# Groups of 256 tokens from the fourth on, and seven products over all 24 inner blocks

## The chip, the cores and the metric

The kernel runs on one core of a Trainium2 chip. The time is the device time of one execution in microseconds, and the time given for a kernel is the median of its runs. One execution is also recorded by the hardware profiler; its span runs from the first to the last instruction.

The core has five engines that run in parallel, each through its own instructions in order. TensorE (PE in the profile; PEld is its weight load) multiplies matrices into PSUM. VectorE (DVE), ScalarE (ACT) and GpSimd (POOL) work elementwise. SyncE (SP) issues DMA transfers and transposes; some transfers are issued from POOL.

## The reference

```python
# attention: q, k, v are (8, 12, 448, 64)
attn = np.maximum(q @ k.T / 8, 0) ** 2 / 448
x    = (attn @ v), heads side by side              # (8, 448, 768)
# mixing and feed-forward
u    = x + real(fft(fft(x, axis=1), axis=2))
un   = (u - mean(u)) / sqrt(var(u) + 1e-6)         # over the last axis
out  = u + np.maximum(un @ w_ch1, 0) @ w_ch2       # w_ch1 (768, 3072), w_ch2 (3072, 768)
```

There are 8 x 448 = 3,584 tokens of 768 channels. The 3,072 inner columns of the feed-forward part are 24 blocks of 128. The inputs and the output are float32; the matmuls take bfloat16 and accumulate in float32.

## The kernel before

**A planner writes the order.** The kernel is a set of Python generators, called streams. Each yields, with `need`, an engine, an estimated duration, the events it depends on (a `Cell` each) and the buffers it takes. `Streams.run` picks the stream that can start first (ties by rank) and lets it emit its instructions. So the order of each engine's instructions is fixed when the program is built, from estimates, and the hardware then runs every engine's list in that order, waiting where a semaphore says so.

**Attention and mixing, batch by batch.** TensorE makes score blocks (L588) into the three double banks `psS`; ACT takes their relu (L612) and VectorE squares them in place (L618); TensorE multiplies four squared blocks with v (L573) into one of the two banks `psF`. VectorE scales the result out of the bank (L474, L478), folds it (L497 to L511), and TensorE applies the Fourier matrices (L1034, L865). q and k of batches 2 and up are copied by VectorE (L412, one buffer each) and transposed by a DMA on SP (L424). The mixed rows u go to memory, their normalised form un too (`n_store`), and a DMA transpose on SP (L971 in `turn_un`) brings un back with channels on partitions, as `unT`. How far attention may run ahead is tied to the progress of the feed-forward part (`lead`, `APART`), so that TensorE always has both kinds of work until the last batch is mixed.

**Feed-forward, group by group.** `GT` cuts the tokens into groups: 384, 512, 384, 512, 256, 512, 512, 512. For a group of N tokens, `ffn` first makes the 24 inner blocks: for each block six matmuls of N columns (L1225) into a `psF` bank, and a relu by ACT (L1203) into `hT`, which has room for 24 x 512 columns and exists once. A bank holds 512 columns, so at N = 256 two blocks share a bank and a relu. When half the blocks are done, the loads of u into the output tiles `o` may start (L1167 in `outputs`, six slots). The second layer multiplies `hT` with the second weights for each tile of 128 tokens and each half of the 768 channels; VectorE adds the result to `o` (L1212), and SP stores `o` (L1171).

**Seven products for eight.** In groups 0 to 2 (`PLAIN`) the second layer is a plain sum over 24 blocks (L1256). From group 3 on it takes two 128-token tiles L and R together, a `Pair`, and treats two tiles by two halves of the inner blocks by two channel halves as a 2 x 2 matrix product that needs seven products instead of eight. An even and an odd inner block form the inner halves, so `KP` = 8 means that 16 of the 24 blocks are handled so; the other 8 are added the plain way (`rest`). A pair thus takes 7 x 8 + 4 x 8 = 88 matmuls of 384 columns (L1312).

This needs sums of rows and sums of weights. `early` makes s1, s2 and a difference in place for each pair on VectorE (L1293, L1295, L1297), in the portions `CH`, as the blocks arrive; `late` (L1305) makes one more, after chain b's first product has read the old value. `weight_sums` makes T1 to T4 once on VectorE (L1115), at the lowest rank; T3 lies in `unT0`, T2 in the former homes of u, T4 in former homes of squares, q and k, and T1 replaces a part of the second weights, so it must wait until group 2 has used them (`w2_free`). s1 and s2 lie in former homes of un, their last portion in `warm`.

`chain_a` and `chain_b` are two streams that alternate on TensorE, one bank each. A product goes into the bank on top of the former ones, and between products VectorE adds the bank's content to one of the `o` tiles. A relu of the next group may write `hT` only after both chains are done.

**Homes of `unT`.** Group 2 is transposed into `unT0`; groups 1 and 3 to 7 use `unT1`, so the transposes for one group wait for the first layer of the group before it. `turn_un(b)` runs inside the stream `mixes`, after the mix of batch b.

Of the kernel before, what the change touches and what calls it, by code (L numbers as in the profile page):

```python
# [142 lines left out]
def kernel(  # L143
# [27 lines left out]
    GT = [0, 384, 896, 1280, 1792, 2048, 2560, 3072, B * S]  # L171
    NGR = len(GT) - 1
    KP = 8
# [791 lines left out]
    def turn_un(b):  # L965

        def turn(g, c0, src, r0, w, deps, bufs=()):
            e = yield need("SP", 1.5, deps, bufs)
            if g is None:
                g = work.tile([128, MC, 512], BF16, name="unT", tag=f"unT{int(len(groups) != 2)}", bufs=1)  # L970
            nc.sync.dma_start_transpose(out=g[:, :, c0:c0 + w], in_=src[r0:r0 + w, :])  # L971
            return g, sch.dma(e + 0.5, w * D * 2, 180e3)

        if b == 1:
            yield need("SP", 0.0, second_un)
            e = max(c.t for c in second_un)
            BUN[0].free.append(e)
            BUN[1].free.append(e)
            group_ready[1].t = e
            return  # L980

        for k in range(2, NGR):
            if (GT[k + 1] - 1) // S != b:
                continue
            t, g = GT[k], None
            while t < GT[k + 1]:
                bb, r = divmod(t, S)
                src, half, r0 = (ntop[bb], 0, r) if r < HS else (nbot[bb], 1, r - HS)
                w = min(HS - r0, GT[k + 1] - t)
                g, e = yield from turn(g, t - GT[k], src, r0, w, n_stored[bb][half::2], [BUNT] if g is None else [])  # L990
                t += w
            groups.append((GT[k], GT[k + 1] - GT[k], g))
            group_ready[k].t = e

# [23 lines left out]
    def mix(b):  # L1018
# [39 lines left out]
        for ch in range(2):  # L1058
            if b > 0:
                sch.add(mix_rows(b, ch, pcs), (1, 1))  # L1060
            else:
                if ch == 0:
                    sch.add(first_tail(pcs), (0, 0))
                sch.add(first_stores(ch), (1, 1))
        if b > 0:
            yield from turn_un(b)
            return
# [13 lines left out]
    CH = [(0, 6), (6, KP)]  # L1081
# [10 lines left out]
    def weight_sums():  # L1092
# [34 lines left out]
        t4 = []  # L1127
        for tag, dep in ((f"sq{NSQ - 2}", sq_left), (f"sq{NSQ - 1}", sq_left), ("qn0", qk_left), ("kn0", qk_left)):
            t4 += yield from home(tag, 2, [dep])
# [50 lines left out]
    def ffn(b):  # L1180
# [4 lines left out]
        h = hid[0]  # L1185
# [22 lines left out]
        def add(pc, e, c, hf, last=True, give=True):  # L1208

            e = yield need("DVE", dve(DH), [e + LATENCY["PE"], ot[b, c, hf]])  # L1210
            o = os[b, c, hf]
            nc.vector.tensor_tensor(o, pc[:, 0:DH], o, op=ALU.add)  # L1212
            if give:
                BF.give(pc, e)
            if last:
                added[b, c, hf].t = e + LATENCY["DVE"]
            return e + LATENCY["DVE"]
# [18 lines left out]
        if b == 2:  # L1236
            unt_left.t = e
        else:
            BUNT.free.append(e)

        if b not in PLAIN:
            for p in pairs:
                sch.add(p.chain_a(), (4, 0))
                sch.add(p.chain_b(), (4, 0))
# [20 lines left out]
    class Pair:  # L1265
# [4 lines left out]
        def __init__(self, b, c, h, ht, add, advance):  # L1270
            self.b, self.c, self.h, self.ht, self.add, self.advance = b, c, h, ht, add, advance
            self.L, self.R = slice(c * 128, c * 128 + 128), slice(c * 128 + 128, c * 128 + 256)
            self.ev = [slice(2 * i0, 2 * i1, 2) for i0, i1 in CH]
            self.od = [slice(2 * i0 + 1, 2 * i1, 2) for i0, i1 in CH]
            self.r12, self.r4 = ([Cell() for _ in CH] for _ in range(2))
            self.m2, self.done = Cell(), [Cell(), Cell()]
            self.reads = Cell(), Cell()
            self.waits, Pair.read = Pair.read, [self.reads[0], self.reads[1], *self.r4]

        def early(self):  # L1280

            h, L, R_ = self.h, self.L, self.R
            if not made:
# [3 lines left out]
                ab = work.tile([128, 2, 2, 128], BF16, name="s3", tag="warm", bufs=1)  # L1287
                made.extend([[a1, ab[:, 0]], [a2, ab[:, 1]]])
# [19 lines left out]
        def product(self, pc, lhs, rhs, start, n=DH):  # L1308

            k = len(lhs)  # L1310
            for i in range(k):
                nc.tensor.matmul(pc[:, 0:n], lhsT=lhs[i], rhs=rhs[i], start=(start and i == 0),  # L1312
                                 stop=(i == k - 1), skip_group_check=True)
            self.advance(k * mm(n))

        def rest(self, pc, cols, hf, start):

            js = range(2 * KP, JC)
            self.product(pc, [self.h[:, j, cols] for j in js], [w2(j, hf) for j in js], start)
# [13 lines left out]
        def chain_a(self):  # L1333

            c, d, dr = self.c, KP * mm(DH), (JC - 2 * KP) * mm(DH)
            s1_read, s2_read = self.reads
            e = yield need("PE", d, self.ht[:2 * KP], [BF])
            pc = BF.take()
            self.product(pc, self.block(0, self.L), self.weights(0, 0), True)
            t = yield from self.add(pc, e, c, 0, False, False)  # L1340
# [3 lines left out]
            t = yield from self.add(pc, e, c + 1, 0, False, False)  # L1344
# [3 lines left out]
            t = yield from self.add(pc, e, c + 1, 1, False, False)  # L1348
# [6 lines left out]
        def chain_b(self):  # L1355

            c, d, dr = self.c, KP * mm(DH), (JC - 2 * KP) * mm(DH)
            e = yield need("PE", d + dr, self.ht, [BF])
            pc = BF.take()
            self.product(pc, self.block(1, self.L), self.weights(1, 0), True)  # L1360
            self.rest(pc, self.L, 0, False)
# [5 lines left out]
            t = yield from self.add(pc, e, c + 1, 1, False, False)  # L1367
            e = yield need("PE", d + dr, [t, sums[4]])
            self.product(pc, self.block(1, self.R), T[4], False)
            self.rest(pc, self.R, 0, False)  # L1370
            yield from self.add(pc, e, c + 1, 0)
            e = yield need("PE", dr, [], [BF])
            pc = BF.take()
            self.rest(pc, self.R, 1, True)
            self.done[1].t = e
            yield from self.add(pc, e, c + 1, 1)
# [20 lines left out]
    with tc.manual_schedule():  # L1397
# [13 lines left out]
        sch.add(weight_sums(), (6, 6))  # L1411
        for slot in range(6):
# [33 lines left out]
```

## Time and profile before

| | before |
|---|---|
| median of 3 runs | 599.19 us (599.04 to 600.49) |
| the profiled execution | 599.02 us |
| its span | 597.2 us |
| granted clock of TensorE | 1.000 |
| busy: PE, DVE, ACT, POOL | 583.0, 390.7, 292.5, 156.4 us |

Group 3's first layer starts at 275.6 us of the span. The last attention work ends near 479 us; what follows is feed-forward alone. In the rows below, a line such as `L1225 PE MATMUL psF<-unT,w 128*128 128x512` is a group of instructions of one source line, engine and shape, with its count, its busy time and the mean duration of one, and after the second bar the idle time before them and what ended it. A row of the chain gives a start, a length and what ran, and the chain follows the work that ended last back in time. A row of waits names who waited for whom: us in total, times, longest. A row of the timeline starts with start and duration.

### The profile page before, as it was taken

Reading aid. Unit: us, or ns where it says so; the run is one execution under the profiler, and the core shown is the slowest. Engines: PE = TensorE matmul, PEld = TensorE weight load, DVE = VectorE, ACT = ScalarE, POOL = GpSimd, SP = SyncE. Lnnn points to the kernel's source line nnn. Section 1 sums busy time; section 2 is a strip of 40 time slices with the busy share of each in tenths; the row PEclk is TensorE's granted clock in tenths of the full one; section 3 lists DMA queues with packets and bytes.
Section 4 is the critical chain, followed back from the end, with each engine's and each line's share of the span. In section 5 each row is a group of like instructions: output and inputs, shape, how many; then the busy total and the mean of one; then the engine's idle time right before and its main releaser. Section 6 shows DMA issues by size and latency. Waiting matters only on the chain.

```text
span 597.2 us, 10407 instructions
## 1 busy us (share of the span) xinstructions
PE 583.0 (98%) x3962; PEld 321.8 (54%) x3982; DVE 390.7 (65%) x889; ACT 292.5 (49%) x433; POOL 156.4 (26%) x200
## 2 busy tenths in 40 slices
PE   8999999989999999999989999999999999999997
PEld 7566556534455565555435667554355544654464
DVE  6977775865587767968857779757967481431043
ACT  5967661568545557534764147546743144004400
POOL 8433112311154135213531145114500062000000
PEclk9999999999999999999999999999999999999999
DMA  9999999974939989996598828974542133422021
GB/s 128 207 209 228 213 218 139 196 106 69 178 109 212 177 108 256 162 159 130 132 169 133 150 108 187 162 141 134 136 92 83 49 125 106 126 69 64 1 70 63
DMA packets 133361, 82.23 MB, mean 138 GB/s; under 512 B 77376, under 2 KB 128480, under 8 KB 133312
## 3 DMA queue, kind: packets, MB, share of 16 engines
q0 software_dynamic: 40320, 34.07, 35.7%
q1 hardware_dynamic: 92992, 47.50, 34.8%
q8 instruction: 31, 0.51, 0.3%
q14 instruction: 18, 0.15, 0.1%
HBM read 62.91 MB, written 26.69 MB: 150 GB/s over the span
## 4 chain that ended last, share of the span: by engine, by line
PE 85%; DVE 6%; ACT 3%; SPq 2%; DMA 2%; issue 1%; POOL 0%; DVEq 0%; ACTq 0%; POOLq 0%
PE psF L1225 32%; PE psF L1312 22%; PE psF L1256 13%; PE psF L573 6%; PE psS L588 6%; PE psS L1034 2%; ACT sq L612 2%; DVE sq L618 2%; PE psS L865 1%; SPq L1167 1%; DMA qkT<-qkr 1%; PE psS L664 1%; DVE stats L900 1%; PE psS L1009 1%; DVE u L887 0%
## 5 line engine op out<-in xcount | busy, mean ns | idle before, releaser
L1225 PE MATMUL psF<-unT,w 128*128 128x512 bf16 (+2 forms) x1132 | 226.2, 352 | 5.4 <-DVE xT L478 2.0
L612 ACT ACTIVATE sq<-psS 112x896 bf16<-112x896 f32 x192 | 164.9, 916 | 84.9 <-PE psS L588 82.0
L1225 PEld LDWEIGHTS <-w 128*128 128x128 bf16 x1152 | 109.4, 98 | 114.0 <-issue 13.9
L1203 ACT ACTIVATE hT<-psF 128x512 bf16<-128x512 f32 (+1 forms) x168 | 96.7, 576 | 127.9 <-PE psF L1225 124.7
L618 DVE TENSOR_TENSOR sq<-sq 112x896 bf16<-112x896 bf16 x192 | 121.9, 651 | 37.5 <-ACT sq L612 36.8
L1212 DVE TENSOR_TENSOR o<-psF,o 128x384 f32<-128x384 f32 x92 | 50.9, 554 | 70.6 <-PE psF L1312 67.6
L1312 PEld LDWEIGHTS <-hT 128*128 128x128 bf16 x648 | 62.9, 98 | 43.6 <-issue 2.1
L1312 PE MATMUL psF<-w,hT 128*128 128x384 bf16 x504 | 85.7, 326 | 0.0
L1256 PE MATMUL psF<-w,hT 128*128 128x384 bf16 x480 | 82.1, 326 | 0.0
L1256 PEld LDWEIGHTS <-hT 128*128 128x128 bf16 x480 | 45.5, 98 | 34.0 <-issue 5.7
L588 PE MATMUL psS<-qkT 64*112 64x448 bf16 x384 | 52.4, 366 | 1.4 <-ACT qkT L452 0.4
L319 POOL DMA_DIRECT2D vn<-in_v_dram x24 | 17.3, 721 | 120.0 <-PE psF L573 108.9
L573 PE MATMUL psF<-sq,vn 112*64 112x448 bf16 x384 | 45.5, 358 | 0.5 <-ACT hT L1203 0.5
L885 POOL TENSOR_TENSOR u<-tp,xn 128x385 f32<-128x385 f32 (+1 forms) x14 | 13.2, 942 | 97.3 <-DVE tp L874 89.8
L474 DVE TENSOR_SCALAR xT<-psF 128x224 bf16<-128x224 f32 x48 | 18.4, 384 | 28.4 <-PE psF L573 28.4
L917 POOL TENSOR_SCALAR un<-u,rstd,nmr 128x768 bf16<-128x768 f32 (+1 forms) x24 | 28.7, 1199 | 28.9 <-DVE nmr L909 26.3
L588 PEld LDWEIGHTS <-qkT 64*112 64x112 bf16 x384 | 20.8, 125 | 26.9 <-issue 21.0
L573 PEld LDWEIGHTS <-vn 112*64 112x64 bf16 x384 | 17.8, 109 | 22.7 <-issue 14.1
L319 POOL DMA_DIRECT2D qn<-in_q_dram x21 | 15.2, 721 | 50.3 <-DVE qkr L412 41.8
L900 DVE BATCH_NORM_STATS2 stats<-u 128x6 f32<-128x384 f32 (+1 forms) x56 | 28.2, 539 | 0.0
L1312 PE MATMUL psF<-wsum,hT 128*128 128x384 bf16 x144 | 26.4, 326 | 0.0
L942 POOL DMA_INDIRECT ubot<-u,back x16 | 16.9, 1056 | 23.9 <-ACT hT L1203 19.7
(137 smaller groups left out, 496.9 us busy)
## 6 DMA issues: line engine op xcount, KB each, us to landing
out_dram<-o SPq DMA_DIRECT2D x56, 192.0 KB
vn<-in_v_dram POOLq DMA_DIRECT2D x24, 224.0 KB, 5.0
qn<-in_q_dram POOLq DMA_DIRECT2D x21, 224.0 KB, 5.0
kn<-in_k_dram POOLq DMA_DIRECT2D x21, 224.0 KB, 6.7
w<-in_moe_w_ch_dram POOLq DMA_DIRECT2D x12, 384.0 KB, 13.8
w<-in_moe_w_ch_dram POOLq DMA_DIRECT2D x4, 1152.0 KB
utop<-u SPq DMA_DIRECT2D x8, 384.0 KB
o<-utop SPq DMA_DIRECT2D x16, 192.0 KB
```

The costliest lines, as they stand in the source:

```text
L319: nc.gpsimd.dma_start(out=t, in_=src[b, hs].rearrange("h (p j) d -> p h (j d)", j=4))
L573: nc.tensor.matmul(av[h * Dh:(h + 1) * Dh, 0:S], lhsT=vn[:, c, h0 + h, :], rhs=sq[:, h, :], start=(c == 0), stop=(c == 3))
L588: nc.tensor.matmul(sc[:R, h, 0:S].rearrange("k (c q) -> k c q", c=4), lhsT=kT[ps, m % 2, c, :], rhs=qT[ps, m % 2], start=True, stop=True)
L612: nc.scalar.activation(r, sc[:R, :, 0:S], AF.Relu)
L618: nc.vector.tensor_tensor(r, r, r, op=ALU.mult)
L900: nc.vector.bn_stats(stats[:n, hf, :], u[:n, hf * (D // 2):(hf + 1) * (D // 2)])
L917: nc.gpsimd.tensor_scalar(un[:n], u[:n], rstd[:n, i:i + 1], nmr[:n, i:i + 1], op0=ALU.mult, op1=ALU.add)
L1203: nc.scalar.activation(hs, ps, AF.Relu)
L1212: nc.vector.tensor_tensor(o, pc[:, 0:DH], o, op=ALU.add)
L1225: nc.tensor.matmul(ph[:, i * N:(i + 1) * N], lhsT=w1_sb[m][hf][:, (jj + i) * 128:(jj + i + 1) * 128], rhs=unT[:, m, 0:N], start=(m == 0), ...
L1256: nc.tensor.matmul(pc[:, 0:DH], lhsT=h[:, j, c * 128:(c + 1) * 128], rhs=w2(j, hf), start=(j == 0), stop=(j == JC - 1))
L1312: nc.tensor.matmul(pc[:, 0:n], lhsT=lhs[i], rhs=rhs[i], start=(start and i == 0), stop=(i == k - 1), skip_group_check=True)
```

## The change

- **Groups.** From token 1,280 on, every group has 256 tokens: nine groups where there were five, twelve groups in all. Each of the nine is one pair.
- **Products.** `KP` = 12: the seven products run over all 24 inner blocks, in three portions (`CH`), and `rest` is gone. A pair takes 7 x 12 = 84 matmuls.
- **The first product of each chain** is split (`first`): nine blocks, then the last three, with the wait for the last relus between them. Chain b starts after chain a's first product.
- **Homes.** In groups of 256 the inner blocks fill half of `hT`. The upper half now holds T4 (12 blocks) and the later portions of s1 and s2. T3 and T2 take the homes that T4 leaves. T4, like T1, now waits until group 2's second layer is done.
- **Transposes of un** run in a stream of their own (`turns`). Groups 3 to 11 use the two halves of `unT1` by turns, so a group's transposes wait for the first layer two groups back, and in the upper half of a batch only for the stores of the rows that they read.

```diff
-    GT = [0, 384, 896, 1280, 1792, 2048, 2560, 3072, B * S]
+    GT = [0, 384, 896] + list(range(1280, B * S + 1, 256))
-    KP = 8
+    KP = 12
...
-    def turn_un(b):
+    def turns():
...
+                n = n_stored[bb]
+                deps = n[1::2] if half else n[0:3:2][int(r0 >= 128):1 + int(r0 + w > 128)]
+                e = yield need("SP", 1.5, deps, [BUNT] if g is None else [])
...
+                    if pair_homes is None:
+                        pair_homes = work.tile([128, 2, MC, 256], BF16, name="unT", tag="unT1", bufs=1)
+                    g = pair_homes[:, k % 2]
+                nc.sync.dma_start_transpose(out=g[:, :, t - GT[k]:t - GT[k] + w], in_=src[r0:r0 + w, :])
...
-    CH = [(0, 6), (6, KP)]
+    CH = [(0, 6), (6, 10), (10, KP)]
+
+    def upper(at, count, width):
+
+        flat = hid[0].rearrange("p j n -> p (j n)")
+        return flat[:, at:at + count * width].rearrange("p (i n) -> p i n", n=width)
...
         t3 = yield from home("unT0", 8, [unt_left] + w2_ready)
+        for i in (2, 1):
+            t3 += yield from home(f"sq{NSQ - i}", 2, [sq_left])
...
+        for x in "qk":
+            t2 += yield from home(f"{x}n0", 2, [qk_left])
...
-        yield from several(4, t4, b21, t2, ALU.subtract, [])
         yield from several(1, b12, b12, b11, ALU.subtract, [w2_free])
+        t4 = upper(JC * 256, KP, DH)
+        yield from several(4, [(t4, i) for i in range(KP)], b21, t2, ALU.subtract, [w2_free])
...
-        h = hid[0]
+        flat = hid[0].rearrange("p j n -> p (j n)")
+        h = hid[0] if b in PLAIN else flat[:, 0:JC * 256].rearrange("p (j n) -> p j n", n=256)
...
+        def first(self, k):
+
+            cut = KP - 3
+            yield need("PE", cut * mm(DH), self.ht[k:2 * cut:2] + [self.m1] * k, [BF])
+            pc = BF.take()
+            self.product(pc, self.block(k, self.L), self.weights(k, 0), True, 0, cut)
+            e = yield need("PE", (KP - cut) * mm(DH), self.ht[2 * cut + k::2])
+            self.product(pc, self.block(k, self.L), self.weights(k, 0), True, cut)
+            return pc, e
...
-            e = yield need("PE", d + dr, [t] + self.r4 + self.ht[2 * KP:])
+            e = yield need("PE", d, [t] + self.r4)
             self.product(pc, self.block(1, self.L), self.weights(1, 1), False)
-            self.rest(pc, self.L, 1, False)
...
-            e = yield need("PE", d + dr, self.ht, [BF])
-            pc = BF.take()
-            self.product(pc, self.block(1, self.L), self.weights(1, 0), True)
-            self.rest(pc, self.L, 0, False)
+            pc, e = yield from self.first(1)
...
+        sch.add(turns(), (1, 1))
```

More of the change, by code (lines that the diff above doesn't have):

```diff
@@ L963, in n_store @@
                 BUN[ch if b < 3 else 0].free.append(n_stored[b][2 * ch + 1].t)
-    def turn_un(b):
[L967 to L980, printed above, removed]
+    def turns():
+        pair_homes = None
         for k in range(2, NGR):
-            if (GT[k + 1] - 1) // S != b:
-                continue
             t, g = GT[k], None
@@ L1306, in late, with product @@
                 self.r4[k].t = e + LATENCY["DVE"]
[L1308 to L1319, printed above, removed]
+        def product(self, pc, lhs, rhs, start, i0=0, i1=KP):
+            for i in range(i0, i1):
+                nc.tensor.matmul(pc[:, 0:DH], lhsT=lhs[i], rhs=rhs[i], start=(start and i == 0),
+                                 stop=(i == KP - 1), skip_group_check=True)
+            self.advance((i1 - i0) * mm(DH))
+        def first(self, k):
[6 more added lines that the diff above has]
+            return pc, e
         def block(self, k, cols):
```

60 lines of the change are left out of this document (32 added, 28 removed).

## The prediction

> **What bounds the kernel now.** I read the page first (busy shares, chain), then the windows and TensorE's waits from group 3 on, then TensorE's groups by form, and last the chain and the VectorE timeline around the stages that change.
>
> ```profile
> span 597.2 us, 10407 instructions
> PE 583.0 (98%) x3962; PEld 321.8 (54%) x3982; DVE 390.7 (65%) x889; ACT 292.5 (49%) x433; POOL 156.4 (26%) x200
> ...
> PE 85%; DVE 6%; ACT 3%; SPq 2%; DMA 2%; issue 1%; POOL 0%; DVEq 0%; ACTq 0%; POOLq 0%
> ```
>
> TensorE is busy 98% of the span and carries 85% of the chain. The first row below is the stretch from group 3's start to the end of the attention work, the second the stretch after it; the columns are length, then busy time of PE, PEld, DVE, ACT, POOL. Then come TensorE's waits in the first.
>
> ```profile
> 276.00:480.00 204.00, 200.94 (x1276) 108.67 (x1283) 147.50 (x332) 101.56 (x149) 54.17 (x54) 1.00 0.63 129
> 480.00:564.80 84.80, 84.54 (x433) 42.68 (x437) 27.10 (x61) 26.43 (x46) 12.29 (x12) 1.00 0.29 86
> ```
> ```profile
> PE psF L1225 <- DVE xT L478: 2.0, 1, 2.0
> PE psF L1225 <- ACT hT L1203: 0.4, 1, 0.4
> PE psF L1225 <- DVE rstd L907: 0.2, 1, 0.2
> ```
>
> TensorE is idle 3.06 us in the first stretch and 0.26 us in the second, 3.3 us in all. So the change is worth what it does to TensorE's own work, plus what happens to these 3.3 us. The clock is 1.00 throughout.
>
> **Prices per matmul.** Three forms matter: the first layer at 512 and at 256 columns, and the second layer.
>
> ```profile
> L1225 PE MATMUL psF<-unT,w 128*128 128x512 bf16 x700 | 159.9, 379 | 5.4 <-DVE xT L478 2.0 <-ACT unT L839 1.7 <-ACT hT L1203 0.4
> L1312 PE MATMUL psF<-w,hT 128*128 128x384 bf16 x504 | 85.7, 326 | 0.0
> L1225 PE MATMUL psF<-unT,w 128*128 128x256 bf16 x144 | 16.7, 273 | 0.0
> ```
>
> The mean ns are latencies of a pipelined engine, so I take the pitch from the chain. In the last group the first layer runs alone from 533.75 to 564.83, and the seven-product part follows it:
>
> ```profile
> 533.75 0.21 PE psF L1225
> ...
> 564.83 28.61 PE psF L1312 x176
> ```
>
> A 512-column group has 24 x 6 = 144 first-layer matmuls (some records are missing from the trace, so I use the program's count): 31.08/144 = 0.2158 us. The second layer: 28.61/176 = 0.1625 us. Group 4 has 256 columns already:
>
> ```profile
> 353.73 1.31 PE psF L1225 x12
> 355.04 0.71 PE psS L588 x6
> 355.75 4.04 PE psF L1225 x36
> ...
> 365.40 0.88 PE psF L573 x8
> 366.28 0.70 PE psS L588 x6
> 366.99 2.73 PE psF L1225 x24
> ```
>
> 1.31/12 = 0.1092 us, and (4.04 - 2.73)/12 = 0.1092 as well; the remaining 0.11 us of each longer piece is paid once after attention work, in a count that hardly changes. I take 0.1092. As a high end, all of group 4's pieces over 144 would be near 0.1134 (the six pieces sum to 16.32 us); as a low end, half a 512-column matmul, 0.1079.
>
> **The change, part by part.** *First layer.* 2,304 tokens ran as four groups of 512 and one of 256; now they run as nine of 256. 576 matmuls of 512 columns become 1,152 of 256: 1152 x 0.1092 - 576 x 0.2158 = 125.8 - 124.3 = +1.5 us (0 at the low end, +6.3 at the high one).
>
> *Second layer.* A pair of 128-token tiles took 7 x 8 products plus 4 x 8 plain matmuls, 88; now 7 x 12 = 84. Nine pairs save 36 x 0.1625 = -5.85 us, all of it on TensorE, which has no slack. Sum: -4.35 us (between -5.85 and +0.45).
>
> *Edges between groups.* There are nine edges into the second layer where there were five. The first product now reads blocks whose last relu comes just before it:
>
> ```profile
> 564.92 0.60 ACT L1203 ACTIVATE hT<-psF 128x512 bf16<-128x512 f32 x1 [0.70 <-PE psF L1225]
> ```
>
> The last first-layer matmul ends at 564.83, so this relu ends 0.69 us later. The change holds three of the twelve blocks back, and the nine before them last 9 x 0.1625 = 1.46 us, so the relu is covered. Then VectorE must make the last third of the sums before the second product, one product per chain later (24 x 0.1625 = 3.9 us after the first layer).
>
> ```profile
> L1293 DVE TENSOR_TENSOR s<-hT 128x768 bf16<-128x768 bf16 x9 | 5.4, 600 | 16.2 <-ACT hT L1203 16.2
> L1293 DVE TENSOR_TENSOR s<-hT 128x256 bf16<-128x256 bf16 x9 | 2.6, 286 | 6.1 <-ACT hT L1203 6.1
> L1212 DVE TENSOR_TENSOR o<-psF,o 128x384 f32<-128x384 f32 x92 | 50.9, 554 | 70.6 <-PE psF L1312 67.6
> ```
>
> The last third is three operations of 0.286 us: done 0.69 + 0.86 = 1.6 us after the first layer if VectorE is free, 2.3 us early. If it is not free, TensorE stands, with everything queued behind it in order. The additions to o (0.554 us) gain cover: a product of 12 lasts 1.95 us instead of 1.30, and a pair has seven additions instead of eight. At the edge back, the next group's first batch needs a bank that chain b freed a product earlier, so I cost it at nothing.
>
> *Weight sums.* They grow from 8 to 12 blocks, and T4 joins T1 behind group 2, because its home is the upper part of hT. Prices by form:
>
> ```profile
> L1115 DVE TENSOR_TENSOR w<-w 128x1152 bf16<-128x1152 bf16 x2 | 1.4, 752 | 0.0
> L1115 DVE TENSOR_TENSOR wsum<-w,wsum 128x768 bf16<-128x768 bf16 x3 | 1.7, 551 | 0.0
> L1115 DVE TENSOR_TENSOR wsum<-w,wsum x5: 353/551/552, 250.3 to 254.3; 128x768 bf16<-128x768 bf16 x3, 128x384 bf16<-128x384 bf16 x2
> ```
>
> In the built order T1 is four operations of 0.752 us and T4 seven (one of 0.752, three of 0.551, three of 0.353): 3.0 + 3.5 = 6.5 us behind group 2, where T1 alone took 1.9 us. T2 and T3 take 13 operations in place of the 12 of T2, T3 and T4, over the same 24 blocks: nothing. These 4.6 us more fall where VectorE also mixes batch 4, and group 3's first layer, which hid them for 42 us, now lasts half as long.
>
> ```profile
> 275.63 1.03 PE psF L1225 x4
> 276.66 1.32 PE psS L865 x8
> ```
> ```profile
> 276.20:296.50 20.30, 20.25 (x108) 9.15 (x108) 17.34 (x38) 13.43 (x23) 10.14 (x10) 1.00 0.57 137
> ```
> ```profile
> 276.21 1.89 DVE L1115 TENSOR_TENSOR w<-w 128x1152 bf16<-128x1152 bf16 x3
> ...
> 287.29 0.95 DVE L618 TENSOR_TENSOR sq<-sq 112x896 bf16<-112x896 bf16 x1 [2.60 <-ACT sq L612]
> ...
> 302.32 0.29 DVE L1293 TENSOR_TENSOR s<-hT 128x256 bf16<-128x256 bf16 x1 [0.50 <-ACT hT L1203]
> ...
> 306.79 0.43 DVE L412 COPY qkr<-kn 112x1024 bf16<-112x1024 bf16 x1 [3.31 <-DMA qkT<-qkr]
> ```
>
> From 275.63, group 3's first layer takes 144 x 0.1092 = 15.7 us, with the batch's row mix (1.32), two score blocks (0.70 each) and one value block (0.88) between, and three re-entries of 0.11: it ends near 295.3, and the second product is due near 299.2. VectorE's work from 276.2 to 296.5 was 17.3 us. Add 4.6 for T, and about 2.7 for the sums of the later blocks and the end of the first third; take off 3.3 that the built order now puts behind them (four row statistics with their aggregates, a fold): 21.3 us, done near 297.5. That leaves 1.7 us of margin, thin but positive, so I cost it at nothing. If VectorE loses more than that, TensorE loses the excess.
>
> *Old wait.* The 2.0 us wait in this stage came from VectorE standing 3.31 us at 306.8 for a transpose of q and k. The built order moves that copy behind group 3's additions, so this stall may go; as others may come, I leave the 3.3 us unchanged, and use them as the bounds of a gain.
>
> *Queues.* SP gets four more transposes (20 for 16), the same stores and as many loads (80 in both orders). Each transpose now waits for the first layer two groups back, not one:
>
> ```profile
> SPq L971 <- PE psF L1225: 12.9, 2, 10.2
> ```
>
> SP stood 10.2 us on one such wait and TensorE lost nothing, so SP's cost is nothing. POOL's queue keeps its order of work. A separate stream for these transposes lets later mixes be placed earlier, but TensorE's built order is the same up to group 2's second layer.
>
> *Sum.* The profiled execution took 599.02 us (597.2 us span and 1.8 us around it), 0.17 below the median: 599.02 - 4.35 + 0.17 = 594.8 us.
>
> **The rivals.** *The idle time goes too.* The built order moves the copy that caused the 2.0 us wait, and the additions have more cover. With all 3.3 us gone: 591.5 us. Against it: VectorE has less slack.
>
> *The gain is eaten.* Each of the six groups beside attention (3 to 8) reaches its second product with VectorE late by 0.5 to 1 us: 3 to 6 us, 598 to 601. The same holds if 256-column matmuls cost 0.1134: +0.45, 599.6. For it: VectorE is busy 147.5 of 204 us there. Against it: 2.3 us of margin at each edge, and group 4's pieces.
>
> *VectorE's queue in group 3 becomes the bound, and the kernel is slower.* The place is the second product of group 3: sums, T4 and T1 all stand in VectorE's order ahead of it. The price is VectorE's delay beyond 1.7 us. One wait like the 3.31 us costs 1.6 us of TensorE's time; it decides once VectorE falls 7.9 us behind, which needs two or three such waits in 20 us: 601 to 604.
>
> *Every matmul carries a large fixed price.* Both widths give the rate per column: (0.2158 - 0.1092)/256 = 0.416 ns, so the fixed part is 0.1092 - 256 x 0.000416 = 2.6 ns. Were it as much as 60 columns, 25 ns, the 540 additional matmuls (4,522 for 3,982) would cost 13.5 us, the columns saved would give 36 x 384 x 0.416 ns = 5.8 back, and the time would be 607 us. The rows leave this little room. The Trainium skill ("TensorEngine Tiling (Array Packing)", Instruction Overhead) states such a rule, that a matmul carries about 60 cycles of overhead on this chip; by that rule the change would lose, and the trace disagrees with it for matmuls of 256 columns and more.
>
> **How the numbers follow.** A measurement of this kernel tells about 0.3%, 1.8 us, from no change. Forecast (593 to 597.2): 0.55. Idle gone too (591 to 593): 0.17. Gain eaten (597.4 to 601): 0.13. Slower through group 3's VectorE queue: 0.12. Fixed price: 0.03. So faster 0.72, same 0.13, slower 0.15. The range runs from the second case's floor (591.4) to where the stalls of the third and fourth reach 5.7 us (600.5).
>
> **What would show it.** Right: one 256-column group with no attention beside it takes 144 x 0.1092 = 15.7 us of first layer and 84 x 0.1625 = 13.65 us of second, 29.4 us; the last two groups of before ((31.08 + 28.60)/2 = 29.8 us per 256 tokens) show the gain at its purest, and 84-matmul pieces stand without gaps. Wrong: TensorE waits on VectorE's sums or additions in groups 3 to 8, a pitch over 0.113 us in the long pieces of the last three groups, or an idle gap before T1, T2 or T4 is first used. What would break the prediction is VectorE's in-order queue, which no row of before shows under this load.

## The result and the profile after

The changed kernel took 594.64 us in the median of six runs (593.83 to 597.21), the kernel before 599.90 us beside it on the same chip (599.04 to 601.02): a ratio of 0.992, with a 95% interval of 0.9894 to 0.9946. It is faster by about 0.8%. The profiled execution took 593.86 us, with a span of 592.1 us.

On the page after, the span, the busy shares and the chain by engine answer to the first rows of before:

```profile
span 592.1 us, 11558 instructions
PE 580.2 (98%) x4522; PEld 374.7 (63%) x4522; DVE 400.9 (68%) x925; ACT 292.7 (49%) x433; POOL 159.0 (27%) x200
...
PE 86%; DVE 7%; ACT 3%; issue 2%; POOL 2%; DMA 0%; DVEq 0%; POOLq 0%; ACTq 0%
```

TensorE still is the bound, with 540 matmuls more by the program's count (560 by these rows, as the records of 20 are missing before) and less time. VectorE has 10 us more work. Weight loads rose by 53 us, and the chain has none of them.

The lines of the code have moved: the first layer is L1240 now (L1225 before), the products L1327 (L1312), the additions to `o` L1226 (L1212), the row sums L1309 to L1313 (L1293 to L1297), the weight sums L1124 (L1115), the relu L1215 (L1203). The edits of the experiments move some of them by one or two more.

The stage that changes runs from the start of group 3's first matmul (275.20 us before, 275.11 after; the chain's piece at 275.63 begins a little later, behind that matmul and a missing record) to the end of the last matmul. Its window before, and then after (length, then busy time of PE, PEld, DVE, ACT, POOL, then the granted clock):

```profile
275.20:593.44 318.24, 314.86 (x1885) 168.77 (x1897) 187.26 (x419) 128.59 (x196) 66.46 (x65) 1.00 0.49 111
```
```profile
275.11:588.54 313.43, 311.91 (x2439) 221.70 (x2437) 197.62 (x455) 128.77 (x196) 69.27 (x66) 1.00 0.53 113
```

The stage is 4.8 us shorter. The feed-forward work in it, by the program's counts and the pitches of the prediction, was 576 x 0.2158 + 144 x 0.1092 + 9 x 88 x 0.1625 = 268.7 us and is 1296 x 0.1092 + 9 x 84 x 0.1625 = 264.4 us, 4.35 us less. All that is left of the stage, attention, mixing and idle time, went from 49.5 to 49.1 us. The rest of the span's 5.1 us, about 0.3 us, lies ahead of group 3 (0.1 us) and behind the last matmul.

The end of the chain after shows the new price of a group:

```profile
500.42 15.72 PE psF L1240 x144
516.14 13.65 PE psF L1327 x84
529.79 15.72 PE psF L1240 x144
```

15.72/144 = 0.1092 us and 13.65/84 = 0.1625 us. Each row begins where the one before it ends, so an edge between the layers costs nothing. 29.37 us per group of 256 tokens, where before took 29.8.

TensorE's waits in this stage after are two:

```profile
PE psF L1327 <- DVE xT L478: 0.7, 1, 0.7
PE psF L1327 <- DVE o L1226: 0.6, 1, 0.6
```

The 2.0 us wait of before is gone. The named waits of the stage fell from 2.6 to 1.4 us, but its other time outside the feed-forward matmuls grew by about 0.8 us. It lies in late starts that the length of the matmul before them hides from the idle time, such as this one in the chain:

```profile
313.95 1.47 PE psF L1240 x12
```

Twelve of these matmuls take 1.31 us where nothing is late. The first of the twelve waited for a relu (L1215), and the trace has four such places after, 0.17 us each, where it has one before; two more products start 0.2 us late on an addition (L1226), at 299.72 and 492.46. Worked out from the starts of all matmuls and the pitches, the late starts of the stage sum to 3.2 us before and 2.9 us after. The first new wait stands in group 3, in the stretch where the prediction gave VectorE a margin of 1.7 us. TensorE's and VectorE's timelines there:

```profile
297.54 2.12 PE L1327 MATMUL psF<-w,hT 128*128 128x384 bf16 x12 [0.72 <-DVE xT L478]
299.72 0.48 PE L1327 MATMUL psF<-wsum,s 128*128 128x384 bf16 x2
```
```profile
287.96 2.29 DVE L1124 TENSOR_TENSOR hT<-w,wsum 128x384 bf16<-128x384 bf16 x6
...
297.11 0.38 DVE L478 TENSOR_SCALAR xT<-psF 128x224 bf16<-128x224 f32 x1
...
297.92 0.28 DVE L1313 TENSOR_TENSOR hT<-hT 128x256 bf16<-128x256 bf16 x1
```

The pair's sums are done at 298.20, and the product that reads them starts at 299.72: the sums came in time. At all nine edges they were done 1.1 us or more ahead of that product, 2.2 us in the last three groups. TensorE stood one product earlier. Chain b's first product needs a `psF` bank, and that bank was held by a value block until VectorE had scaled it out (L478), which stood in the same queue behind the work for T4, T1 and the sums. Two operations in this stretch also took twice their time, beside work of POOL (first VectorE, then POOL):

```profile
292.19 1.32 DVE L618 TENSOR_TENSOR sq<-sq 112x896 bf16<-112x896 bf16 x1
...
294.82 1.26 DVE L618 TENSOR_TENSOR sq<-sq 112x896 bf16<-112x896 bf16 x1
```
```profile
293.12 1.50 POOL L885 TENSOR_TENSOR u<-tp,xn 112x385 f32<-112x385 f32 x1
294.58 1.02 POOL L887 TENSOR_TENSOR u<-qs,xn 112x383 f32<-112x383 f32 x1
```

None of the 132 operations of L618 in this trace that have no instruction of POOL beside them took more than 0.63 us.

### The profile page after: what moved, and what is told of

It is laid out like the page before. It is cut to its first block, busy times and chain, and to the rows that moved or that the text cites. A ratio compares the mean times of both kernels' runs of the same rounds, so it can differ in the third digit from the quotient of the medians.

```text
span 592.1 us, 11558 instructions
## 1 busy us (share of the span) xinstructions
PE 580.2 (98%) x4522; PEld 374.7 (63%) x4522; DVE 400.9 (68%) x925; ACT 292.7 (49%) x433; POOL 159.0 (27%) x200
## 4 chain that ended last, share of the span: by engine, by line
PE 86%; DVE 7%; ACT 3%; issue 2%; POOL 2%; DMA 0%; DVEq 0%; POOLq 0%; ACTq 0%
PE psF L1240 34%; PE psF L1327 19%; PE psF L1271 13%; PE psS L588 7%; PE psF L573 7%; PE psS L1036 2%; ACT sq L612 2%; DVE sq L618 1%; PE psS L865 1%; PE psS L664 1%; POOL un L917 1%; DVE stats L900 1%; PE psS L1011 1%; DVE o L1226 1%; DVE u L887 0%
## 5 line engine op out<-in xcount | busy, mean ns | idle before, releaser
L1240 PE MATMUL psF<-unT,w 128*128 128x256 bf16 (+2 forms) x1728 | 229.3, 291 | 1.8 <-ACT unT L839 1.7
L1240 PEld LDWEIGHTS <-w 128*128 128x128 bf16 x1728 | 165.7, 98 | 61.9 <-issue 15.2
L1215 ACT ACTIVATE hT<-psF 128x512 bf16<-128x512 f32 (+1 forms) x168 | 96.7, 576 | 118.1 <-PE psF L1240 116.0
L618 DVE TENSOR_TENSOR sq<-sq 112x896 bf16<-112x896 bf16 x192 | 119.1, 633 | 36.0 <-ACT sq L612 35.3
L1327 PEld LDWEIGHTS <-hT 128*128 128x128 bf16 x648 | 62.9, 98 | 43.6 <-issue 2.2
L1271 PE MATMUL psF<-w,hT 128*128 128x384 bf16 x480 | 82.1, 326 | 0.0
L1226 DVE TENSOR_TENSOR o<-psF,o 128x384 f32<-128x384 f32 x83 | 45.8, 552 | 45.8 <-PE psF L1327 40.7
L1327 PE MATMUL psF<-w,hT 128*128 128x384 bf16 x378 | 66.4, 326 | 1.4 <-DVE xT L478 0.7
L474 DVE TENSOR_SCALAR xT<-psF 128x224 bf16<-128x224 f32 x48 | 18.6, 388 | 29.7 <-PE psF L573 29.6
L1327 PE MATMUL psF<-wsum,hT 128*128 128x384 bf16 x162 | 28.6, 326 | 0.0
L942 POOL DMA_INDIRECT ubot<-u,back x16 | 18.2, 1140 | 26.3 <-ACT sq L612 21.8
```

The costliest lines, as they stand in the source:

```text
L618: nc.vector.tensor_tensor(r, r, r, op=ALU.mult)
L1215: nc.scalar.activation(hs, ps, AF.Relu)
L1240: nc.tensor.matmul(ph[:, i * N:(i + 1) * N], lhsT=w1_sb[m][hf][:, (jj + i) * 128:(jj + i + 1) * 128], rhs=unT[:, m, 0:N], start=(m == 0), ...
L1271: nc.tensor.matmul(pc[:, 0:DH], lhsT=h[:, j, c * 128:(c + 1) * 128], rhs=w2(j, hf), start=(j == 0), stop=(j == JC - 1))
L1327: nc.tensor.matmul(pc[:, 0:DH], lhsT=lhs[i], rhs=rhs[i], start=(start and i == 0), stop=(i == KP - 1), skip_group_check=True)
```

## The experiments

All the edits are made on the changed kernel. "The stage" is always the stretch from group 3's first matmul to the end of the last one, 313.43 us after; its lengths come from the traces, medians and ratios (to the kernel before on the same chip) from the timed runs.

**The same kernel again.** Not edited, it gives the spread.

> The changed kernel unaltered, on the chip and beside the runs of before that the next three share: 0.990 to 0.995 of before, and from group 3's first matmul to the last one 313 to 314 us.

595.48 us (595.18 to 597.09), ratio 0.9927 [0.9902, 0.9952]. The stage took 313.33 us, the same to 0.1. The profiled span is 1.5 us longer all the same: that time lies ahead of the stage (the last experiment below takes it up).

**Eight blocks in the products again**, with groups, homes and transposes as after. It tells the work from everything else.

```diff
-    KP = 12
+    KP = 8
...
-    CH = [(0, 6), (6, 10), (10, KP)]
+    CH = [(0, 6), (6, KP)]
...
-            pc, e = yield from self.first(0)
-            self.m1.t = e
+            e = yield need("PE", d, self.ht[:2 * KP], [BF])
+            pc = BF.take()
+            self.product(pc, self.block(0, self.L), self.weights(0, 0), True)
...
+            self.rest(pc, self.L, 1, False)
```

> The changed kernel with only 16 of the 24 inner blocks in the seven products again (88 matmuls a pair instead of 84); groups of 256, homes and the stream of transposes stay. If the gain is TensorE's own work: 36 x 0.1625 = 5.85 us slower than the changed kernel, 599.5 to 600.5 us, so about level with before (first layer +1.5, old 2.0 us wait gone). If the gain came from the new groups, homes and transposes (less idle time): within 2 us of the changed kernel, 594 to 596.

602.59 us (600.59 to 603.33), ratio 1.003 [1.0013, 1.0047]: slower than before. That is 2 us above the expected range; two of its ten runs had a clock of 1.000, and these took 600.6 and 600.8 us. The last groups in the chain (L1335 is `rest`):

```profile
553.22 2.60 PE psF L1327 x16
...
567.52 15.72 PE psF L1240 x144
```

The second layer of a pair takes 14.30 us here (553.22 to 567.52), 88 matmuls at 0.1625, and 13.65 after: 0.65 us for each of nine pairs, 5.85 us. The stage took 318.9 us; in this order a row mix (1.3 us) lies ahead of it and a score block (0.7 us) is in it that after has outside, so 319.5 us for the same work, 6.1 more than after. 5.85 of them are these matmuls. Against before, this kernel has the +1.5 us of the narrow groups and nothing that pays for it, and its stage is 1.3 us longer than before's. So the gain is the saved products; the smaller groups, the homes and the separate transposes bring none of their own.

**The first product in one piece.** The planner may place a chain's first product only when all relus are made. It tests what holding three blocks back is worth.

```diff
-            yield need("PE", cut * mm(DH), self.ht[k:2 * cut:2] + [self.m1] * k, [BF])
+            e = yield need("PE", KP * mm(DH), self.ht[k::2] + [self.m1] * k, [BF])
             pc = BF.take()
-            self.product(pc, self.block(k, self.L), self.weights(k, 0), True, 0, cut)
-            e = yield need("PE", (KP - cut) * mm(DH), self.ht[2 * cut + k::2])
-            self.product(pc, self.block(k, self.L), self.weights(k, 0), True, cut)
+            self.product(pc, self.block(k, self.L), self.weights(k, 0), True)
```

> The changed kernel with the first product of each chain in one piece, so that it waits for all its relus. If the held-back three blocks cover the relu: the relu ends 0.69 us after the last first-layer matmul, so TensorE stands about 0.7 us at each edge with nothing else to do; in the last three groups that is 2.1 us, and where attention work lies between the first layer and the product it costs nothing: 2 to 5 us slower, 596 to 599, and the last three groups take 30.1 us each instead of 29.4. If the relu is hidden anyway: no change, 29.4 us.

597.51 us, ratio 0.9964 [0.9939, 0.9989]. The time is in the range expected if the held-back blocks matter, but not for that reason: the dearer last groups that were expected did not come. Chain, then the waits in the stage:

```profile
503.11 15.72 PE psF L1240 x144
518.83 13.65 PE psF L1327 x84
```
```profile
PE psF L1327 <- DVE o L1226: 1.7, 3, 0.7
PE psF L1327 <- DVE xT L478: 1.3, 2, 0.7
PE psS L588 <- DMA qkT<-qkr: 0.5, 1, 0.5
```

With no attention beside them the groups still take 29.37 us. So the split in the program is not what covers the last relu. The stage is 2.3 us longer, and all of that lies beside attention, where TensorE now stands 3.5 us in place of 1.4: the planner, told of a later start, built another order of TensorE's, VectorE's and ACT's instructions. What covers the relu is tested next.

**One piece, read from the last block to the first.** On top of the last edit, so that the block with the last relu is read first.

```diff
+                at = KP - 1 - i if last_first else i
-                nc.tensor.matmul(pc[:, 0:DH], lhsT=lhs[i], rhs=rhs[i], start=(start and i == 0),
+                nc.tensor.matmul(pc[:, 0:DH], lhsT=lhs[at], rhs=rhs[at], start=(start and i == 0),
...
+            self.product(pc, self.block(k, self.L), self.weights(k, 0), True, 0, KP, True)
```

> The first product of each chain in one piece, as in the run of that name, and its twelve blocks in reverse, emitted after all relus: its first weight load needs the last relu. If the blocks ahead of the last relu's block are what covers it: TensorE stands 0.7 us at every edge of the last three groups, 30.1 us a group instead of 29.37, about 2 us slower than in one piece without the reversal. If the relu is hidden by something else: 29.37 us.

602.13 us, ratio 1.0033 [1.0017, 1.0049]. The chain at an edge:

```profile
536.08 15.73 PE psF L1240 x144
551.90 0.60 ACT hT L1215
552.50 0.05 issue
552.55 13.82 PE psF L1328 x84
```

From the end of the first layer (551.81) TensorE stands 0.74 us until the relu is made, and the products take 0.17 us longer, so a group takes 30.3 us. Every engine has the same order of instructions as in the run before, and the stage is 5.4 us longer than there, 0.9 us at each of the last four edges and the rest beside attention. So it is the order in which the blocks are read that hides the relu: TensorE waits only at the block that needs it.

**The same reversal with the split kept.**

> The changed kernel with the first product of each chain taking its twelve blocks in reverse, so that its first matmul needs the last relu of the group; planner's estimates and order of streams stay. If the nine blocks ahead of the last three are what covers the relu: TensorE stands 0.7 to 0.8 us between first and second layer wherever nothing lies between; the last three groups take 30.1 us instead of 29.4, 2 to 5 us slower in all. If the relu is hidden by something else: 29.4 us, no change.

595.40 us, ratio 0.9918 [0.9888, 0.9947]. This run says nothing of the edge. Here the first nine products stand ahead of the last relus in the program, so they take what these blocks held before, TensorE waits for none, and the values of the last relus are left out of the first product.

**T4 behind the first pair's sums.** It takes seven VectorE operations out of the thin stretch of group 3.

```diff
-        yield from several(4, [(t4, i) for i in range(KP)], b21, t2, ALU.subtract, [w2_free])
+        yield from several(4, [(t4, i) for i in range(KP)], b21, t2, ALU.subtract, [w2_free, sums_made])
...
+            sums_made.t = sums_made.t or e
```

> The changed kernel with T4 made only after the sums of the first pair in VectorE's order. If T4's 3 us ahead of group 3's sums cause the 0.72 us wait at group 3's second chain: that wait goes, up to 0.7 us faster, 593 to 594, and the first pair's sums end 2 to 3 us earlier. If T4 is then late for its own product: TensorE waits on it 1 to 3 us there, 595 to 597.

598.52 us, ratio 0.9968 [0.995, 0.9987]. The waits in the stage:

```profile
PE psF L1328 <- DVE xT L478: 2.2, 1, 2.2
PE psF L1240 <- DVE xT L478: 0.9, 1, 0.9
PE psF L573 <- DVE o L1226: 0.6, 1, 0.6
PE psF L1328 <- DVE o L1226: 0.6, 1, 0.6
```

Neither expectation held. Nothing waited for T4, and the stage is 2.9 us longer, with 4.3 us of waits in place of 1.4. They are of the kind that after has already, for banks that VectorE empties late, at other places: the edit let the planner build another order. It can't tell what T4 costs where it stands, so the next two keep the order and add time.

**More VectorE time at T4's place, which the planner isn't told of.** All seven operations of T4 issued twice (3.0 us by their prices), and three of the seven (1.46 us by their prices):

```diff
-                nc.vector.tensor_tensor(a, b, c, op=op)
+                for _ in range(2 if n == 4 else 1):
+                    nc.vector.tensor_tensor(a, b, c, op=op)
```
```diff
+                for _ in range(2 if n == 4 and i1 in (4, 6, 8) else 1):
```

> The changed kernel with each of T4's operations issued twice in a row, without telling the planner, so that every engine's order stays and VectorE has 3.0 us more to do ahead of group 3's second chain. The profile of the changed kernel shows TensorE waiting 0.72 us there, on VectorE's scaling of the last value block. If VectorE's queue is already the bound at that place, all of it comes through: 2.3 to 3.0 us slower than the changed kernel, in one longer wait at group 3. If the margin of 1.7 us of the prediction is there: 0.6 to 1.3 us slower. If VectorE catches up in idle time: no change.

> As the run with T4 twice, but only three of its seven operations are issued twice: 1.46 us more for VectorE ahead of group 3's second chain. If VectorE's delay comes through one to one and the larger loss with 3.0 us came from the clock: TensorE's waits at group 3 grow from 0.7 to about 2.1 us, the clock stays 1.00 there, and from group 3's first matmul to the last one it takes 314.5 to 315 us instead of 313.3. If each us of VectorE costs nearly two in itself: 316 us. If there is slack: 313.3 us.

With three doubled: 596.13 us, ratio 0.9929 [0.9908, 0.995], a stage of 314.54 us, 1.1 more than after. TensorE's timeline in group 3, and VectorE's row of T4, which in after is the one at 287.96 (2.29 us):

```profile
296.76 0.38 PE L573 MATMUL psF<-sq,vn 112*64 112x448 bf16 x2 [1.04 <-DVE sq L618]
...
300.50 2.12 PE L1328 MATMUL psF<-w,hT 128*128 128x384 bf16 x12 [0.60 <-DVE xT L478]
```
```profile
289.80 6.36 DVE L1125 TENSOR_TENSOR hT<-w,wsum 128x384 bf16<-128x384 bf16 x9
```

1.64 us of waits here in place of 0.72, less than the 2.1 expected, and a clock of 1.00 as expected. The three operations cost VectorE 4.1 us and not their price: some of T4's took 1.0 to 1.3 us each, beside work of POOL. Behind T4 VectorE makes up for most of that, because after has 0.89 us of idle time and the two stretched L618 and a stretched row sum (L1311) there, and this run has neither. Counted from the start of the stage, the scaling (L478) that chain b waits for starts at 23.1 us (300.06 - 276.95), where after has it at 22.0 (297.11 - 275.11). VectorE is 1.1 us late there and the stage is 1.1 us longer: at this place no margin is left.

With all seven doubled: 600.01 us, ratio 0.9992 [0.9972, 1.0012], a stage of 318.90 us, 5.5 more than after. TensorE's timeline, VectorE's row of T4, and the windows at the wait and behind it (the number after the last bracket is the granted clock):

```profile
298.82 0.58 PE L573 MATMUL psF<-sq,vn 112*64 112x448 bf16 x2 [3.11 <-DVE sq L618]
```
```profile
290.45 7.78 DVE L1125 TENSOR_TENSOR hT<-w,wsum 128x384 bf16<-128x384 bf16 x12
```
```profile
294.92:298.33 3.41, 0.79 (x7) 0.36 (x7) 3.31 (x8) 0.60 (x1) 2.59 (x3) 1.00 0.16 58
298.33:305.16 6.83, 6.34 (x23) 2.77 (x23) 6.30 (x16) 2.53 (x3) 0.00 (x0) 0.50 0.53 126
```

The long wait stands at a value block ahead of chain b now. Counted from the start of the stage, VectorE comes to the squares of this block (L618) 6.3 us later than after (298.15 - 276.81 against 290.17 - 275.11), and TensorE waits 3.11 us, so this block had about 3 us of slack; with three doubled it was 4.1 us and 1.04. TensorE's waits in group 3 grew by 3.11 - 0.72 = 2.4 us. Then the clock stands at 0.50 for 6.83 us, which costs half of the 6.34 us that TensorE works in them, 3.2 us. Together that is 5.6 us, the whole difference, and more than any of the expectations. Two of the ten runs took 598.0 and 598.2 us at a mean clock of 0.997, the others 599.5 to 602.0 us at 0.988 to 0.994, so the clock does not take as much from each run.

**The transposes in one home of `unT`**, so that they wait for the first layer of the group before.

```diff
-                    g = pair_homes[:, k % 2]
+                    g = pair_homes[:, 0]
...
-            BUNT.free.extend([e, e] if b == 1 else [e])
+            BUNT.free.append(e)
```

> The changed kernel with one home of unT for groups 3 to 11 instead of two, so that a group's transposes wait for the first layer of the group before. If the transposes are hidden as SP's 10 us waits were in before: they have the 13.65 us of a second layer, and TensorE waits on none of them; time within 2 us of the changed kernel, as the planner's order shifts. If they take longer than a second layer: a wait on a transpose of 1 to 5 us at each of the last edges, 598 to 608.

596.79 us, ratio 0.9956 [0.9932, 0.9979]; the stage took 314.8 us, 315.4 for the same work (a row mix lies ahead of it and a score block more in it, as with eight blocks), 2.0 more than after. The waits of SP's queue (SPq) for the first layer, first after, then here:

```profile
SPq L983 <- PE psF L1240: 13.6, 2, 10.5
```
```profile
SPq L983 <- PE psF L1240: 29.2, 6, 11.9
```

SP stands twice as long for the home, and no matmul waits for a transpose, so these are hidden with one home as with two. What TensorE lost is again the order's:

```profile
PE psF L1327 <- DVE xT L478: 1.9, 1, 1.9
PE psF L1327 <- DVE o L1226: 1.3, 2, 0.6
```

**The last group's first layer in matmuls of 128 columns**, 288 in place of 144. It measures the fixed price of a matmul and whether its weight load limits it.

```diff
+                w = 128 if b == NGR - 1 else N
+                for c0 in range(0, N, w):
...
+                                         rhs=unT[:, m, c0:c0 + w], start=(m == 0), stop=(m == MC - 1))
```

> The changed kernel with the last group's first layer in matmuls of 128 columns: 288 instead of 144, in a stage with nothing beside it. If only the fixed 2.6 ns per matmul counts: 288 x 0.056 = 16.1 us instead of 15.7, 0.4 us slower. If the weight load of 98 ns sets the pitch as soon as the columns stream faster than it: 288 x 0.100 = 29 us, 13 us slower, about 607. If each matmul costs 25 ns beside its columns: 288 x 0.078 = 22.6 us, 7 us slower, about 601.

595.84 us in a single run. The chain's row, and the groups of these matmuls and of their weight loads in the last group:

```profile
560.81 16.08 PE psF L1242 x288
```
```profile
L1242 PE MATMUL psF<-unT,w 128*128 128x128 bf16 x288 | 16.2, 219 | 0.0
L1242 PEld LDWEIGHTS <-w 128*128 128x128 bf16 x288 | 16.2, 98 | 0.1
```

16.08 us where 15.72 stood: 144 matmuls more cost 0.36 us, 2.5 ns each, so the fixed price that the prediction worked out of two widths (2.6 ns) holds at a third. The pitch is 0.0558 us although each matmul has a weight load of its own of 98 ns: loads overlap with matmuls and with each other, and their duration does not limit the pitch here. The Trainium skill ("TensorE: Matmul & The Clock Gate", Back-to-back issue gap) gives N/2.4 + 2.5 ns for an isolated matmul, and for pairs of load and matmul about 81 ns at 128 columns and about 131 ns at 512. The trace disagrees with the figures for pairs (55.8 and 215.8 ns) and agrees with the formula.

**Matmuls on zeroes in the gap at 122 us.** 28 matmuls of 128 columns between the last turning of batch 1's rows and group 1's first layer. The executions of one kernel differ by about 1.5 us a step, and a clock of 0.997 or 0.994 goes with the longer ones; the two traces of the changed kernel differ in this place.

```diff
+        for _ in range(28 if done is second_un[4] else 0):
+            nc.tensor.matmul(pt[:, 0, 384:512], lhsT=warm[:, 0:128], rhs=warm[:, 0:128], start=True, stop=True)
```

> The changed kernel with 28 matmuls of 128 columns on zeroes between the last transposes of batch 1's rows and group 1's first layer (about 124 us), where TensorE waits 1.73 us for ACT in every run and the clock falls to half for 3 us in some. If the steps of 1.6 us between runs of one kernel come from that place: every run shows clock 0.999 or more and 593.8 to 594.2 us, at or below the lowest of the changed kernel, median 0.5 to 1.5 us lower. If they come from elsewhere: the same steps as before, median 594.6 to 595.5.

594.36 us (594.35 to 594.52), ratio 0.9905 [0.9888, 0.9922]. The spread of the runs is 0.17 us, where the changed kernel has 3.4 us on one chip and 1.9 us on another; on the chip of this run, the one with three of T4's operations doubled has 1.7 us (595.21 to 596.95). The window of group 1's first matmuls in the profiled execution after, and two windows of the same kernel's second trace, that of the first experiment:

```profile
124.10:128.00 3.90, 3.84 (x24) 1.67 (x25) 0.77 (x3) 1.20 (x3) 0.00 (x0) 1.00 0.96 97
```
```profile
120.42:123.83 3.41, 1.81 (x18) 0.89 (x15) 3.38 (x10) 3.04 (x5) 0.00 (x0) 1.00 0.35 94
123.83:127.25 3.42, 2.86 (x7) 1.02 (x7) 1.10 (x3) 0.55 (x2) 0.00 (x0) 0.50 1.13 113
```

Ahead of group 1's first matmul TensorE stands 1.73 us in one wait in both. In one execution the clock stays at 1.00, in the other it is 0.50 for 3.4 us, which costs half of the 2.86 us that TensorE works in them, 1.4 us. With the additional matmuls the wait is 0.74 us, and none of the four runs lost the 1.4 us:

```profile
122.26 1.73 PE L837 MATMUL psS<-warm 128*128 128x128 bf16 x28
124.73 1.46 PE L1242 MATMUL psF<-unT,w 128*128 128x512 bf16 x6 [0.74 <-ACT unT L841]
```

They cost 0.5 us against the fastest run of the changed kernel (593.83). The median is 0.3 us below that kernel's, less than the 0.5 to 1.5 us expected, and the two intervals overlap, so this is a steadier kernel and not shown to be a faster one.

## Why the prediction was right, and where it was not

The forecast was 594.8 us, the median is 594.64.

- **The sum was right, term by term.** The pitches hold to a hundredth of a microsecond over whole groups, so the first layer's +1.5 us and the second's -5.85 us are what the stage shows; with eight blocks put back, 5.85 of the 6.1 us return. The profiled execution is 0.8 us below the sum made against its own time (599.02 - 4.35 = 594.67), by 0.5 us inside the stage and 0.3 outside it. That the medians agree to 0.2 us is partly luck: some executions of either kernel carry about 1.5 us of lost clock or a multiple of it.
- **Edges at nothing: right**, since nine blocks ahead of the last relu outlast it. The prediction laid this to the change that holds three blocks back. The one-piece run shows that their place in the order of reading does it, and the split matters to the planner alone. The sums were in time at all nine edges, by 2.2 us in the last three, where 2.3 was forecast. The additions to `o` were to gain cover, and that was wrong: TensorE waited 0.65 us for one and 0.2 us for two more, and in before for none.
- **Transposes, SP's queue at nothing: right.** SP can wait twice as long without a matmul noticing.
- **The old wait may go and others may come: right.** 3.3 us were left unchanged as a whole; the stage's time outside the feed-forward work fell by 0.5 us. The size of 3.3 us was right by luck. About 0.7 us of it was no idle time: at 14 places the record of a first-layer matmul is missing, which leaves a gap of 0.05 us each. And the idle time leaves out about as much in late starts, which sum to 3.2 us before and 2.9 after. The rival in which the idle time goes too had half of its mechanism (the 2.0 us wait did go) and did not get its time.
- **"1.7 us of margin" in group 3: the step that was mis-sized.** The sums came at 298.2, where 297.5 was forecast, and the second product read them in time. But I looked only at the sums. The bank of chain b's first product hangs on the same VectorE queue, one product earlier, and was late by 0.72 us. The margin was gone, as the run with three of T4's operations doubled shows, so the forecast came out because little more was late. Operations that took twice their time beside POOL are part of VectorE's lateness; how much of it was not isolated.
- **The slower rival had its place right and its price too low.** It was to cost VectorE's delay beyond 1.7 us, and to decide at 7.9 us. At the scaling that chain b waits for the delay costs from the start, and after a stand of 3.11 us the clock took 3.2 us more: with T4 made twice, VectorE was 6.3 us late at the squares, less than the 7.9, and the kernel was where before is (0.9992). The prediction had no term for the clock, which was 1.00 in all rows that it had read.
- **"Gain eaten" by 0.1134 us a matmul, or by a large fixed price: refuted**, by 0.1092 us in all the last groups and 0.0558 us at 128 columns.

Still open: the three edits that moved the planner's order (one piece, T4 late, one home) each lost 2.0 to 2.9 us with the same matmuls; that the order does it is argued from their waits, but which choice of the planner is at fault was not isolated.

## What to carry to other kernels

Where one engine is busy 98% of the span, count its instructions, take the pitch from long unbroken rows of the chain and not from the mean of one, and the sum holds to a few tenths of a microsecond in 300. A margin at a busy in-order engine has to be taken for everything in its queue that the bound engine waits for, banks being emptied as well as operands being made. And when a program's order comes from a planner, an experiment that changes a dependency also changes the order: to price a delay, add work that the planner isn't told of, and read in the trace how long that work took there.

## What was not expected of the hardware

- **The clock falls after short stands, and not in each execution.** A stand of 3.11 us was followed by 6.83 us at 0.50. At 124 us, a stand of 1.73 us, with shorter ones ahead of it, was followed by 3.41 us at 0.50 in one execution and by 1.00 in another. In each of the 13 traces the clock's record changes only after whole multiples of 3.413 us, and the grid of these steps lies at another place of the program in each execution. The nearest step lay within 0.6 us of the end of the 1.73 us stand in the seven traces that lost the clock there, and 1.3 to 1.9 us behind it in the five that did not (the trace with the additional matmuls is not counted). So the place of the grid went with the loss in all twelve; what about the window decides it is not shown. The Trainium skill ("TensorE: Matmul & The Clock Gate", "What's actually happening") says that the clock is halved after an idle window of about 3.4 us, and that the windows run free of the program. The traces agree with the length and with the windows running free. They disagree with the window being idle: in the 3.41 us ahead of the two falls shown above TensorE was busy for 0.79 and 1.81 us.
- **28 matmuls on zeroes, 1.73 us of work, took the spread of the runs from 1.9 to 3.4 us down to 0.17 us**, in four runs. So one step of 1.4 us comes from this place. There are others: the trace with eight blocks, at a mean clock of 0.993, is at 0.50 near 54 us as well as near 125 us.
- **Some of VectorE's operations take twice as long and more beside POOL.** In all 13 traces together, L618, which squares in place in SBUF, took at most 0.63 us in the 1,773 cases with no instruction of POOL beside it; of the 723 with one, 93 took over 0.65 us and the longest 2.2 us. The additions (L1226) and scalings (L474, L478), which read a PSUM bank, never took longer beside POOL than else (at most 0.56 and 0.39 us). The cause was not tested.
- **A weight load of 98 ns goes with a matmul every 55.8 ns.** In the last group 288 loads in place of 144 cost the chain no more than the fixed price of their matmuls.
